# Start-up of a fused convolution and gated feed-forward kernel: w_out scaled on VectorE, w_in loaded for both halves, fp32r remainder of the taps, fillers in the first spread, moved casts, transposes and taps

## Chip, cores, metric

One core of a Trainium2 chip. The metric is the device time of one execution in microseconds (us), lower is better. All runs are compared with runs of the kernel before taken on the same chip in turn.

Three readings of the trace are used throughout, besides the total:

- **T0**: start of the first Silu instruction (ScalarE) of step 0.
- **T1**: start of the first Silu of step 1. Step 0 and step 1 each have 16 half-width Silus.
- **T2**: start of the first full-width Silu, the first of step 2.

## The reference

```python
# x: (8, 4096, 192); weight: (8 heads, 7 taps); w_in: (192, 2048); w_out: (2048, 192)
w = softmax(weight, axis=-1)                 # per head
x_pad = concat([zeros(8, 6, 192), x], axis=1)
conv = sum over k of w[head, k] * x_pad[:, s + k, channels of head]
h = conv.reshape(32768, 192) @ w_in
g = h * sigmoid(beta * h)
out = g @ w_out                              # (32768, 192) float32
```

## The kernel before

Tokens are worked in steps: two of 256 columns (steps 0 and 1), then 31 of 512, each for two halves of the batch at once. In each step a loop over 16 blocks `fc` of the 2048 hidden units issues `hidden` (TensorE, then Silu on ScalarE) for this step and `output` (TensorE) for the step before. Silu is computed as silu(beta h), so w_out is scaled by 1/beta once. VectorE computes the convolution of step s+2 meanwhile: 21 instructions ("taps") per step, taken one by one from a queue at a rate that `pops` sets. The convolutions of steps 0 and 1 are done on TensorE instead, with diagonal matrices, because VectorE would be too late for them. TensorE writes its results to PSUM, a small memory of its own; the kernel takes PSUM in tiles from two pools (`ph` and `po`) of two tiles each, so TensorE must wait when both tiles of a pool are still in use.

```python
w_in_s = consts.tile([128, NG, F], BF16)
def load_w_in(i):                       # to the lower 64 partitions
    nc.gpsimd.dma_start(out=w_in_s[0:DG, :, cols], in_=...)
def copy_w_in(i):                       # to the upper 64
    nc.vector.tensor_copy(w_in_s[DG : 2 * DG, :, cols], w_in_s[0:DG, :, cols])
...
def spread(dst, sel, e8):               # exp(weights), one head a row, to 128 partitions
    for c in range(NG):
        nc.tensor.matmul(dst[...], sel[:, c], e8, start=True, stop=True)
...
fill(5)                                 # matmuls of zeros, to keep TensorE busy
spread(pc[:, 0, :], sel_r, e8r)         # rounded (fp32r) taps, for the diagonal matrices
fill(1)
nc.vector.tensor_copy(eu..., pc[...])
...
def taps():                             # exact taps, for VectorE's convolution
    spread(pq, sel, e8)                 # fp32
    ...
def prep_w_out(c0, n):
    nc.gpsimd.tensor_tensor(w_out_s[...], w_out_raw[...], beta_r[...], ALU.mult)
cast(2)
for c in range(0, NF, 4):
    prep_w_out(c, 4)
cast(3)
...
first_work = {                          # extra work of step 0, by fc
    0: lambda: (first_xt(), taps()),
    2: lambda: (more(xt1_work)(), copy_w_in(1)),   # transposes of the second chunk
    4: lambda: (more(xt1_work)(), copy_w_in(2)),
    6: lambda: (more(conv1_work)(), copy_w_in(3)), # 7 matmuls of step 1's convolution
    8: more(conv1_work),
    11: more(conv1_work),
}
pops = {1: 12, 2: 26}
for s in range(N_ST + 1):
    if s + 2 < N_ST:
        queue.extend(conv_ops(s + 2))
    for u in range(NF):
        if s < N_ST: hidden(s, u)
        if s > 0: output(s - 1, u)
        if s == 0 and u in first_work: first_work[u]()
        n = pops.get(s, 24)
        pops_u = (u + 1) * n // NF - u * n // NF if s else u > 5
        for _ in range(pops_u):
            if queue: queue.popleft()()
        ...
```

## Time and profile before

| | kernel before |
|---|---|
| median of the first 3 runs | 696.64 us |
| profiled span | 695.1 us |
| T0, T1, T2 | 11.84, 25.60, 37.18 us |
| TensorE busy | 687.6 us (99%) |

Busy time of the engines by stage (columns: stage, its length, then busy us and instruction count of each engine). From 60 to 680 us TensorE has no idle time at all, and the change leaves those stages and the last 15 us alone, so only what happens before 60 us can show a difference:

```profile
core 0: us, PE busy (x) PEld busy (x) DVE busy (x) ACT busy (x) POOL busy (x), PEclk, DMA share, GB/s
...
12.00:28.00 16.00, 14.60 (x213) 11.29 (x209) 14.21 (x19) 12.59 (x20) 12.72 (x12) 1.00 1.35 188
28.00:40.00 12.00, 11.68 (x215) 9.90 (x213) 11.93 (x22) 10.97 (x16) 7.01 (x8) 1.00 2.05 155
...
60.00:680.00 620.00, 620.00 (x10440) 474.00 (x10436) 494.01 (x837) 529.06 (x475) 29.87 (x33) 1.00 0.45 70
```

ScalarE's instructions in order of time, merged where they follow each other (columns: start, length, engine and line, operation, shapes, count, and in brackets the idle time before the group and what ended it):

```profile
11.84 0.69 ACT L402 ACTIVATE g<-ph,beta 128x512 bf16<-128x512 f32 x1 [0.37 <-PE ph L395]
13.49 2.55 ACT L402 ACTIVATE g<-ph,beta 128x512 bf16<-128x512 f32 x4 [0.97 <-PE ph L395]
16.25 1.27 ACT L402 ACTIVATE g<-ph,beta 128x512 bf16<-128x512 f32 x2 [0.21 <-PE ph L395]
18.09 1.43 ACT L402 ACTIVATE g<-ph,beta 128x512 bf16<-128x512 f32 x2 [0.57 <-PE ph L395]
20.30 1.97 ACT L402 ACTIVATE g<-ph,beta 128x512 bf16<-128x512 f32 x3 [0.78 <-PE ph L395]
23.05 13.11 ACT L402 ACTIVATE g<-ph,beta 128x512 bf16<-128x512 f32 x20 [0.78 <-PE ph L395]
37.18 5.17 ACT L402 ACTIVATE g<-ph,beta 128x1024 bf16<-128x1024 f32 x5 [1.02 <-PE ph L395]
```

Step 0 is 16 Silus with five gaps; each gap is TensorE doing something else first. Step 1 has no gap; then comes one of 1.02 us. What that one waits for is seen on VectorE, in the same form:

```profile
16.80 3.04 DVE L172 COPY w_in_s<-w_in_s 64x1536 bf16<-64x1536 bf16 x2
19.88 2.92 DVE L376 TENSOR_SCALAR ct<-xt,cw 128x512 bf16<-128x512 bf16 x3
...
31.52 0.55 DVE L456 COPY osb<-po 128x384 f32<-128x384 f32 x1
32.11 0.56 DVE L457 TENSOR_TENSOR osb<-po,osb 128x384 f32<-128x384 f32 x1
32.58 4.06 DVE L378 SCALAR_TENSOR_TENSOR ct<-xt,cw,ct 128x512 bf16<-128x512 bf16 x6
```

The six taps that end at 36.64 are the last of step 2's convolution, and step 2's first matmuls wait for them. Two copies at 16.80 take 3.04 us where one takes 0.69 elsewhere, and three first taps take 2.92 where one takes 0.35: they run beside GpSimd's scaling of w_out (four instructions of 1.57 us, 16.2 to 22.4).

The start of the chain is TensorE's (the first spread is L209, the diagonal matmuls of step 0 are L256):

```profile
3.51 0.80 PE L209 MATMUL po<-e8r,sel_r 8*128 8x8 f32 x3
4.24 0.61 PE L205 MATMUL ph<-zeros 128*128 128x512 bf16 x1
...
6.35 3.36 PE L256 MATMUL ph<-xt_145,diag 128*128 128x256 f32 x14
...
9.85 1.10 PE L256 MATMUL po<-xt_145,diag 128*128 128x256 f32 x7
```

Fourteen matmuls take 0.24 us each, the next seven 0.15: the trace's first record of the full TensorE clock is at 9.90 us. The page's own clock column (PEclk) shows 1.00 from the start, because nothing is recorded before that moment; the matmuls' pace shows that it isn't so.

### The profile page before, as it was taken

What the parts mean: (1) busy time and instruction counts of PE and PEld (TensorE: products, weight loads), DVE (VectorE), ACT (ScalarE), POOL (GpSimd) and SP (SyncE); (2) the same over time, 40 slices, a digit from 0 to 9 for tenths busy, and PEclk for the clock granted to TensorE, in tenths of its full rate; (3) what the DMA queues carried; (4) which work ended last, traced back from release to release, by engine and by line L of the source; (5) the groups of instructions that cost most, each with busy time, mean ns of one, the idle gap of its engine ahead of it and who ended that gap; (6) DMA issues with size and microseconds to landing.
All of it is one profiled execution on the core that took longest, in us unless ns stands there. A gap on an engine that the chain in (4) does not pass through costs nothing.

```text
span 695.1 us, 24865 instructions
## 1 busy us (share of the span) xinstructions
PE 687.6 (99%) x11467; PEld 526.6 (76%) x11467; DVE 551.4 (79%) x938; ACT 580.0 (83%) x546; POOL 70.0 (10%) x83
## 2 busy tenths in 40 slices
PE   9999999999999999999999999999999999999997
PEld 6867777777777777777777777777777777777777
DVE  5999998998777987777987777987778987777222
ACT  6898888888888888888888888888888888888881
POOL 7934455000000000000000000000000000000000
PEclk9999999999999999999999999999999999999999
DMA  9999999922232022222023222032222122211012
GB/s 193 144 159 159 168 177 171 123 63 70 54 65 71 27 68 72 47 70 70 26 71 70 49 70 70 25 71 70 48 71 55 40 70 71 48 48 48 25 48 70
DMA packets 181497, 54.57 MB, mean 79 GB/s; under 512 B 146432, under 2 KB 181072, under 8 KB 181392
## 3 DMA queue, kind: packets, MB, share of 16 engines
q0 software_dynamic: 98048, 14.89, 29.8%
q1 hardware_dynamic: 83296, 38.09, 23.9%
q8 instruction: 89, 1.46, 0.9%
q14 instruction: 16, 0.13, 0.1%
q10 hardware_dynamic: 48, 0.01, 0.0%
HBM read 28.98 MB, written 37.29 MB: 95 GB/s over the span
## 4 chain that ended last, share of the span: by engine, by line
PE 96%; DVE 3%; ACT 0%; issue 0%
PE po L442 48%; PE ph L395 46%; DVE ct L378 2%; PE ph L256 0%; DVE w_in_s L172 0%; DVE ct L376 0%; PE ph L205 0%; PE po L209 0%; PE po L243 0%; ACT g L402 0%; PE po L256 0%; DVE xt L346 0%; DVE osb L457 0%; DVE ct L327 0%; ACT xt_145 L269 0%
## 5 line engine op out<-in xcount | busy, mean ns | idle before, releaser
L402 ACT ACTIVATE g<-ph,beta 128x1024 bf16<-128x1024 f32 (+1 forms) x528 | 572.7, 1090 | 96.7 <-PE ph L395 92.6
L442 PEld LDWEIGHTS <-g 64*128 64x128 bf16 x8192 | 369.2, 94 | 101.9
L442 PE MATMUL po<-w_out_s,g 64*128 64x192 bf16 x8192 | 429.8, 243 | 0.0
L395 PE MATMUL ph<-ct,w_in_s 64*128 64x512 bf16 (+1 forms) x3168 | 426.2, 370 | 2.0 <-ACT g L402 1.1
L378 DVE SCALAR_TENSOR_TENSOR ct<-xt,cw,ct 128x512 bf16<-128x512 bf16 x558 | 379.4, 745 | 0.0
L395 PEld LDWEIGHTS <-w_in_s 64*128 64x128 bf16 x3168 | 162.5, 94 | 56.4 <-issue 2.9
L456 DVE COPY osb<-po 128x384 f32<-128x384 f32 x127 | 70.8, 558 | 126.9 <-PE po L442 120.7
L457 DVE TENSOR_TENSOR osb<-po,osb 128x384 f32<-128x384 f32 x129 | 71.5, 555 | 6.0 <-ACT osb L454 1.6
L95 POOL DMA_DIRECT2D xd<-in_x_dram x60 | 54.4, 909 | 46.1 <-DMA xd<-in_x_dram 42.3
L376 DVE TENSOR_SCALAR ct<-xt,cw 128x512 bf16<-128x512 bf16 x93 | 29.5, 372 | 0.0
L454 ACT COPY osb<-po 128x192 f32<-128x192 f32 x2 | 0.6, 320 | 9.9 <-PE po L442 9.9
L352 POOL TENSOR_TENSOR w_out_s<-w_out_raw,beta_r 128x768 bf16<-128x768 f32 x4 | 6.2, 1568 | 2.5 <-DMA w_out_raw<-in_moe_w_out_dram 2.5
L205 PE MATMUL ph<-zeros 128*128 128x512 bf16 x7 | 3.5, 623 | 1.3 <-DVE warm L129 1.3
L172 DVE COPY w_in_s<-w_in_s 64x1536 bf16<-64x1536 bf16 x4 | 4.4, 1121 | 0.1
L256 PE MATMUL po<-xt_145,diag 128*128 128x256 f32 x28 | 4.4, 296 | 0.0
L256 PEld LDWEIGHTS po<-xt_145,diag 128*128 128x128 f32 x28 | 3.6, 189 | 0.7 <-issue 0.6
L256 PEld LDWEIGHTS ph<-xt_145,diag 128*128 128x128 f32 x14 | 3.1, 327 | 0.6 <-ACT xt_145 L269 0.6
L256 PE MATMUL ph<-xt_145,diag 128*128 128x256 f32 x14 | 3.4, 427 | 0.1
L185 POOL DMA_DIRECT2D w_out_raw<-in_moe_w_out_dram x4 | 3.1, 771 | 0.3 <-DMA x1b<-in_x_dram 0.3
L295 ACT ACTIVATE ct<-po,rn 128x256 bf16<-128x256 f32 x1 | 0.5, 475 | 2.6 <-PE po L256 2.6
L165 POOL DMA_DIRECT2D w_in_s<-in_moe_w_in_dram x4 | 2.7, 669 | 0.0
L205 PEld LDWEIGHTS <-zeros 128*128 128x128 bf16 x7 | 0.8, 126 | 2.3 <-DVE warm L129 1.3
(51 smaller groups left out, 28.1 us busy)
## 6 DMA issues: line engine op xcount, KB each, us to landing
out_dram<-osb SPq DMA_DIRECT2D x60, 384.0 KB, 3.1
xd<-in_x_dram POOLq DMA_DIRECT2D x54, 198.0 KB, 14.5
w_out_raw<-in_moe_w_out_dram POOLq DMA_DIRECT2D x4, 384.0 KB, 9.4
out_dram<-osb SPq DMA_DIRECT2D x7, 192.0 KB, 3.7
xd<-in_x_dram POOLq DMA_DIRECT2D x6, 192.0 KB, 13.7
x_83<-in_x_dram SPq DMA_DIRECT2D x4, 192.0 KB, 2.9
w_in_s<-in_moe_w_in_dram POOLq DMA_DIRECT2D x4, 192.0 KB, 7.7
xt<-xd SPq DMA_TRANSPOSE x30, 5.1
```

The costliest lines, as they stand in the source:

```text
L95: nc.gpsimd.dma_start(out=xd[r0:, :, h, :], in_=x_v[p, t0:t1, h, :].rearrange("t (c d) -> t c d", c=NG),)
L172: nc.vector.tensor_copy(w_in_s[DG : 2 * DG, :, cols], w_in_s[0:DG, :, cols])
L205: nc.tensor.matmul(pf[:, 0, :], zeros[:, 0:128], zeros, start=True, stop=True)
L256: nc.tensor.matmul(pv, diag[:, c, k, :], xt0[:, c, o : o + n], start=(k == 0), stop=(k == K - 1),)
L352: nc.gpsimd.tensor_tensor(w_out_s[:, c0 : c0 + n, :], w_out_raw[:, c0 : c0 + n, :], beta_r[:, c0 : c0 + n].unsqueeze(2).to_broadcast((128, ...
L376: nc.vector.tensor_scalar_mul(dst, src, scalar)
L378: nc.vector.scalar_tensor_tensor(out=dst, in0=src, scalar=scalar, in1=dst, op0=ALU.mult, op1=ALU.add)
L395: nc.tensor.matmul(ph[:, h, 0:n], w_in_s[rows, j, cols], cts[s][rows, j, 0:n], start=(j == 0), stop=(j == NG - 1),)
L402: nc.scalar.activation(gs[s][:, fc, :, 0:n], ph[:, :, 0:n], AF.Silu, scale=beta[:, fc : fc + 1])
L442: nc.tensor.matmul(po[:, r, b * D : (b + 1) * D], g[rows, fc, h, q * BLK : (q + 1) * BLK], w_out_s[rows, fc, :], start=(fc == 0), stop=(fc ...
L456: nc.vector.tensor_copy(dst, po[:, 0, cols])
L457: nc.vector.tensor_tensor(dst, po[:, 1, cols], dst, ALU.add)
```

## The change

Its intent is to relieve VectorE and ScalarE in the start-up: GpSimd no longer computes beside VectorE (it goes on issuing DMAs), two of VectorE's four w_in copies become DMA, the exact taps come from cheap fp32r matmuls on the remainder e8 - e8r, added to the rounded taps, the late x rows are cast where VectorE idles, and the first spread is kept "busy" by three small matmuls of zeros ("fillers"). The same edit rearranges step 0: the second chunk's transposes move from fc 2 and 4 to fc 1 and 2, and VectorE takes 7 taps from the queue in step 0 (10 before) and 15 in step 1 (12 before). So 13 of step 2's 21 taps stand ahead of step 1's first output copy, where 15 did.

```diff
-    def load_w_in(i):
+    def load_w_in(i, h=0):
...
-    for i in range(1, NW):
-        load_w_in(i)
+    load_w_in(1)
+    for i in range(2, NW):
+        for h in range(2):
+            load_w_in(i, h)
...
-    def spread(dst, sel, e8):
+    def spread(dst, sel, e8, between=0):
         for c in range(NG):
+            fill(between, 128)
...
+    e8l = setup.tile([H, K + 1], FP32R)
+    nc.vector.tensor_tensor(e8l, e8, e8r.bitcast(FP32), ALU.subtract)
     fill(5)
-    spread(pc[:, 0, :], sel_r, e8r)
+    spread(pc[:, 0, :], sel_r, e8r, between=1)
...
     diag_v(1)
+    nc.vector.tensor_copy(x0b[:, HB:NB], x0[:, HB:NB])
...
-        spread(pq, sel, e8)
+        spread(pq, sel_r, e8l)
+        ef = setup.tile([128, NG, K + 1], FP32)
+        nc.vector.tensor_tensor(ef, pq..., eu, ALU.add)
...
-        nc.gpsimd.tensor_tensor(          # w_out scaling
+        nc.vector.tensor_tensor(
...
     first_work = {
-        0: lambda: (first_xt(), taps()),
-        2: lambda: (more(xt1_work)(), copy_w_in(1)),
-        4: lambda: (more(xt1_work)(), copy_w_in(2)),
-        6: lambda: (more(conv1_work)(), copy_w_in(3)),
-        8: more(conv1_work),
-        11: more(conv1_work),
+        (0, 0): lambda: (first_xt(), taps()),
+        (0, 1): lambda: (more(xt1_work)(), copy_w_in(1)),
+        (0, 2): more(xt1_work),
+        (0, 5): more(conv1_work),
+        (0, 6): lambda: cast(3),
+        (0, 8): more(conv1_work),
+        (0, 11): lambda: (prep_w_out(0), prep_w_out(4), more(conv1_work)()),
+        (0, 13): lambda: prep_w_out(8),
+        (0, 14): lambda: prep_w_out(12),
+        (0, 15): lambda: cast(4),
     }
-    pops = {1: 12, 2: 26}
+    pops = {1: 15, 2: 24}
...
-            pops_u = (u + 1) * n // NF - u * n // NF if s else u > 5
+            pops_u = (u + 1) * n // NF - u * n // NF if s else 2 < u < 10
```

More of the change, by code (lines that the diff above doesn't have):

```diff
@@ L161 @@
     w_in_s = consts.tile([128, NG, F], BF16)
-    def load_w_in(i):
+    def load_w_in(i, h=0):
         cols = slice(i * FW, (i + 1) * FW)
         nc.gpsimd.dma_start(
-            out=w_in_s[0:DG, :, cols],
+            out=w_in_s[h * DG : (h + 1) * DG, :, cols],
             in_=moe_w_in[:, cols].rearrange("(c d) f -> d c f", c=NG),
@@ L201, with fill @@
     pf = psum_h.tile([128, 2, TOK], FP32, name="ph")
-    def fill(n):
+    def fill(n, cols=TOK):
         for _ in range(n):
-            nc.tensor.matmul(pf[:, 0, :], zeros[:, 0:128], zeros, start=True, stop=True)
-    def spread(dst, sel, e8):
+            nc.tensor.matmul(
+                pf[:, 0, 0:cols], zeros[:, 0:128], zeros[:, 0:cols], start=True, stop=True
+            )
+    def spread(dst, sel, e8, between=0):
         for c in range(NG):
+            fill(between, 128)
             nc.tensor.matmul(
@@ L295 @@
             nc.scalar.mul(ct[:, c, 0:n0], pv, rn[:, c : c + 1])
-    beta_r = setup.tile([128, NF], FP32)
-    nc.vector.reciprocal(beta_r, beta)
-    nc.vector.tensor_copy(x0b[:, HB:NB], x0[:, HB:NB])
     cw = consts.tile([128, NG, K], FP32)
@@ L304, in taps @@
         pq = psum_o.tile([128, 2, TOK], FP32, name="po")[:, 0, 0 : NG * (K + 1)]
-        spread(pq, sel, e8)
-        pq = pq.rearrange("p (c k) -> p c k", c=NG)
+        spread(pq, sel_r, e8l)
+        ef = setup.tile([128, NG, K + 1], FP32)
+        nc.vector.tensor_tensor(ef, pq.rearrange("p (c k) -> p c k", c=NG), eu, ALU.add)
         rq = setup.tile([128, NG], FP32)
-        nc.vector.reciprocal(rq, pq[:, :, K])
+        nc.vector.reciprocal(rq, ef[:, :, K])
         nc.vector.tensor_tensor(
-            cw, pq[:, :, 0:K], rq.unsqueeze(2).to_broadcast((128, NG, K)), ALU.mult
+            cw, ef[:, :, 0:K], rq.unsqueeze(2).to_broadcast((128, NG, K)), ALU.mult
         )
@@ L349, with prep_w_out @@
     w_out_s = consts.tile([128, NF, D], BF16)
-    def prep_w_out(c0, n):
-        nc.gpsimd.tensor_tensor(
-            w_out_s[:, c0 : c0 + n, :],
-            w_out_raw[:, c0 : c0 + n, :],
-            beta_r[:, c0 : c0 + n].unsqueeze(2).to_broadcast((128, n, D)),
+    beta_r = setup.tile([128, NF], FP32)
+    def prep_w_out(c):
+        if c == 0:
+            nc.vector.reciprocal(beta_r, beta)
+        nc.vector.tensor_tensor(
+            w_out_s[:, c : c + 4, :],
+            w_out_raw[:, c : c + 4, :],
+            beta_r[:, c : c + 4].unsqueeze(2).to_broadcast((128, 4, D)),
             ALU.mult,
@@ L359 @@
     cast(2)
-    for c in range(0, NF, 4):
-        prep_w_out(c, 4)
-    cast(3)
     def conv_ops(s):
@@ L486 @@
                 output(s - 1, u)
-            if s == 0 and u in first_work:
-                first_work[u]()
+            if (s, u) in first_work:
+                first_work[s, u]()
             n = pops.get(s, 24)
-            pops_u = (u + 1) * n // NF - u * n // NF if s else u > 5
+            pops_u = (u + 1) * n // NF - u * n // NF if s else 2 < u < 10
             for _ in range(pops_u):
@@ L493 @@
                     queue.popleft()()
-            if u == 0 and s + 4 < N_CH:
+            if u == 0 and 0 < s < N_CH - 4:
                 cast(s + 4)
```

## The prediction

> **What bounds it now.** TensorE is busy for 687.6 of 695.1 us, and from 60 to 680 us for all of every window (busy time by stage). The change leaves those stages alone; only the start-up counts. From the instructions in order of time:
> - The first Silu starts at 11.84 us. The 32 half-width Silus of the first two steps take 0.66 us each.
> - Step 0 (16 Silus) lasts until 25.60: 16 x 0.65 plus ScalarE gaps of 0.97, 0.21, 0.57, 0.78, 0.78 us. The last three follow blocks of seven convolution matmuls (1.05 us).
> - Step 1 runs at 0.657 us per Silu to 36.15, then ScalarE idles 0.96 us: step 2's hidden matmuls wait for VectorE's last convolution tap (done 36.64).
> - Step 2 is ScalarE's (1.014 us each), to 53.4; then TensorE's.
>
> So at most 4-5 us can be had, 0.7%.
>
> **What the change does, costed.**
> 1. w_out scaling leaves GpSimd (4 x 1.57 us, 16.2 to 22.4). Meanwhile two w_in copies took 1.43 and 1.68 us instead of 0.69, and two k=0 taps 1.18 and 1.55 instead of 0.29. The Trainium skill ("SBUF — State Buffer", shared port pair) says that GpSimd and a VectorE instruction in a two-port mode exclude each other; this trace agrees, with about 3.9 us lost. VectorE pays instead 4 x about 0.9 us (estimate from diag, 896 fp32 elements in 1.06 us).
> 2. Two w_in copies (0.69 each undisturbed) go; two loads of 192 KB come. Estimate: w_out and the first cast land about 2 us later, still before use.
> 3. The exact taps: six fp32 passes (0.76 us) become three fp32r matmuls, about 0.4 us at full clock, shortening the 0.97 gap by 0.4. Two small VectorE additions: 0.3 us.
> 4. Three fillers in the first spread: eu about 0.2 us later, at half clock. But the granted clock reaches full only at 9.90 us, after 14 diagonal matmuls at 0.24 us instead of 0.15. "TensorE: Matmul & The Clock Gate", Part 1, says that a busy window of about 3.4 us lifts the gate. If the fillers make an earlier window count, about 1.0 us is saved; I give that 40%.
> 5. The late x cast moves into a gap at 7.14-8.25: nothing, since the transposes did not wait for it.
>
> **On the critical path.** VectorE's relief is 3.5-4 us net, but most of it does not arrive. VectorE will reach step 1's first output copy before TensorE has finished that output (start of step 1 + 4.9 us), wait about 1 us, and then still have that pair (1.06) and 8 taps (0.66 each), part of which stood ahead of it before. So step 2 starts about 11.8 us after step 1, against 11.58 now: the stall there stays, with another cause. Step 0 gets about 0.5 us shorter, mostly from item 3. Item 4 is worth -0.2 to +1.0. Sum: 0.2 to 1.8 us gained, about 0.9.
>
> **Predicted: 695.7 us, range 694.0 to 697.0.** Faster by over 2%: 0.005; within 2%: 0.99; slower by over 2%: 0.005.
>
> **What would show it.** Copies and k=0 taps at 0.69 and 0.29 us throughout; w_out scaling 0.9 us on VectorE; the taps' spread near 0.4 us; ScalarE's three conv gaps still 0.6-0.8; the first 1024-wide Silu at about 36.3 (now 37.18) after ScalarE idled near 1 us; VectorE idle before the first output copy; full clock at 6.5 (gain) or 9.9 us; the stages from 60 us equal.
>
> **What would make it wrong.** VectorE reaching that copy late, so that the relief pays in full: 693-694. Or the extra loads and earlier casts delaying a transposed x chunk that step 1 or 2 needs: 697-698. Or the clock gate opening later, by its own phase.

## The result and the profile after

| | before | after |
|---|---|---|
| median (range), 4 runs each | 696.43 us (696.14 to 696.79) | 697.58 us (697.48 to 698.66) |
| profiled span | 695.1 us | 697.0 us |
| eu (rounded taps copied on VectorE) | 4.35 us | 5.06 us |
| first record of the full clock | 9.90 us | 11.56 us |
| T0 | 11.84 us | 12.98 us |
| T1 - T0 | 13.76 us | 14.17 us |
| T2 - T1 | 11.58 us | 11.92 us |
| T2 to the end | 657.9 us | 657.9 us |

The ratio is 1.002 with an interval of 1.0002 to 1.0037: slower by about 1.2 us, which is clear of noise. Ratios here are the mean time of one kernel's runs over that of the other's of the same rounds, so not quite the ratio of the medians quoted. The predicted 695.7 us (694.0 to 697.0) was wrong in size and in sign.

In the two profiled runs T2 is 1.89 us later, and the rest is the same, so all of the loss lies before T2. First the busy time by stage of the changed kernel; the long stage is as full as before, the stages from 12 to 40 us are emptier on TensorE:

```profile
12.00:28.00 16.00, 13.55 (x187) 10.09 (x188) 12.98 (x22) 11.79 (x19) 12.16 (x14) 1.00 1.84 215
28.00:40.00 12.00, 11.39 (x225) 10.31 (x222) 10.67 (x19) 10.66 (x16) 3.94 (x5) 1.00 1.79 157
...
60.00:680.00 620.00, 620.00 (x10434) 475.06 (x10430) 497.40 (x842) 528.49 (x475) 28.91 (x32) 1.00 0.44 70
```

TensorE's start in the changed kernel (L214 is the spread, L207 the fillers, L263 the diagonal matmuls):

```profile
3.61 0.37 PE L214 MATMUL po<-e8r,sel_r 8*128 8x8 f32 x1
3.92 0.29 PE L207 MATMUL ph<-zeros 128*128 128x128 bf16 x1
4.13 0.37 PE L214 MATMUL po<-e8r,sel_r 8*128 8x8 f32 x1
4.44 0.29 PE L207 MATMUL ph<-zeros 128*128 128x128 bf16 x1
4.66 0.37 PE L214 MATMUL po<-e8r,sel_r 8*128 8x8 f32 x1
4.96 0.61 PE L207 MATMUL ph<-zeros 128*128 128x512 bf16 x1
...
7.07 3.36 PE L263 MATMUL ph<-xt,diag 128*128 128x256 f32 x14
```

A spread matmul followed by a filler takes 0.52 us, where spread matmuls alone followed each other at 0.22 to 0.24. The diagonal matmuls start at 7.07 us instead of 6.35. Then ScalarE:

```profile
12.98 0.69 ACT L408 ACTIVATE g<-ph,beta 128x512 bf16<-128x512 f32 x1 [0.37 <-PE ph L401]
14.30 0.69 ACT L408 ACTIVATE g<-ph,beta 128x512 bf16<-128x512 f32 x1 [0.63 <-PE ph L401]
15.46 0.69 ACT L408 ACTIVATE g<-ph,beta 128x512 bf16<-128x512 f32 x1 [0.47 <-PE ph L401]
16.34 1.97 ACT L408 ACTIVATE g<-ph,beta 128x512 bf16<-128x512 f32 x3 [0.20 <-PE ph L401]
19.09 1.97 ACT L408 ACTIVATE g<-ph,beta 128x512 bf16<-128x512 f32 x3 [0.78 <-PE ph L401]
21.84 1.97 ACT L408 ACTIVATE g<-ph,beta 128x512 bf16<-128x512 f32 x3 [0.79 <-PE ph L401]
24.59 9.82 ACT L408 ACTIVATE g<-ph,beta 128x512 bf16<-128x512 f32 x15 [0.78 <-PE ph L401]
35.16 3.32 ACT L408 ACTIVATE g<-ph,beta 128x512 bf16<-128x512 f32 x5 [0.74 <-PE ph L401]
39.07 3.14 ACT L408 ACTIVATE g<-ph,beta 128x1024 bf16<-128x1024 f32 x3 [0.60 <-PE ph L401]
```

The first gap of step 0 shrank from 0.97 to 0.63 us, as the three fp32r passes promised, but a gap of 0.47 us is new and the first convolution gap grew from 0.57 to 0.78. The gap of 0.74 us at 35.16 follows a stall of 0.54 us on TensorE in step 1 (to 34.29) whose cause the trace does not name; a second profile of the same kernel (e5_again) has no such stall and the same T2 - T1, so it cost nothing. And VectorE:

```profile
20.98 1.83 DVE L361 TENSOR_TENSOR w_out_s<-w_out_raw,beta_r 128x768 bf16<-128x768 f32 x2
...
26.76 4.06 DVE L384 SCALAR_TENSOR_TENSOR ct<-xt,cw,ct 128x512 bf16<-128x512 bf16 x6
32.08 0.56 DVE L462 COPY osb<-po 128x384 f32<-128x384 f32 x1 [1.26 <-PE po L448]
32.68 0.56 DVE L463 TENSOR_TENSOR osb<-po,osb 128x384 f32<-128x384 f32 x1
33.15 5.38 DVE L384 SCALAR_TENSOR_TENSOR ct<-xt,cw,ct 128x512 bf16<-128x512 bf16 x8
```

VectorE now stands idle for 1.26 us before the first output copy of step 1, with eight taps still to come behind it that need nothing of that copy. Before, six stood behind it and there was no idle time before it. The eight end at 38.53, and step 2's first matmuls start at 38.58: T2 waits for them.

How much VectorE was relieved can be added up. From T0 to the end of step 2's last tap VectorE was busy for 22.81 us before and 22.21 us after (`--windows 11.84:36.64` and `--windows 12.98:38.53`). So the relief is 0.60 us net: the contention and two copies went, but four scalings of 0.95 us came. Its idle time in that stretch grew from 1.99 to 3.34 us.

### The profile page after: what moved, and what is told of

It reads as the page before. It is cut to its first block, busy times and chain, and to the rows that moved or that the text cites. A ratio compares the mean times of both kernels' runs of the same rounds, so it can differ in the third digit from the quotient of the medians.

```text
span 697.0 us, 24867 instructions
## 1 busy us (share of the span) xinstructions
PE 688.4 (99%) x11467; PEld 528.5 (76%) x11467; DVE 551.2 (79%) x942; ACT 579.5 (83%) x546; POOL 65.0 (9%) x81
## 3 DMA queue, kind: packets, MB, share of 16 engines
q8 instruction: 89, 1.46, 0.9%
## 4 chain that ended last, share of the span: by engine, by line
PE 97%; DVE 1%; ACT 1%; issue 0%
PE po L448 48%; PE ph L401 47%; DVE ct L384 1%; PE po L263 1%; ACT g L408 1%; PE ph L207 0%; PE ph L263 0%; PE po L250 0%; DVE xt L323 0%; DVE osb L463 0%; PE po L214 0%; ACT xt L276 0%; DVE osb L462 0%; ACT ct L303 0%; ACT osb L460 0%
## 5 line engine op out<-in xcount | busy, mean ns | idle before, releaser
L207 PE MATMUL ph<-zeros 128*128 128x512 bf16 (+1 forms) x10 | 4.2, 525 | 1.3 <-DVE warm L129 1.3
L263 PE MATMUL po<-xt,diag 128*128 128x256 f32 x28 | 4.8, 316 | 0.0
L263 PEld LDWEIGHTS po<-xt,diag 128*128 128x128 f32 x28 | 4.0, 211 | 0.7 <-issue 0.6
L361 DVE TENSOR_TENSOR w_out_s<-w_out_raw,beta_r 128x768 bf16<-128x768 f32 x4 | 3.6, 953 | 0.0
L263 PEld LDWEIGHTS ph<-xt,diag 128*128 128x128 f32 x14 | 3.1, 328 | 0.6 <-ACT xt L276 0.6
L263 PE MATMUL ph<-xt,diag 128*128 128x256 f32 x14 | 3.4, 427 | 0.1
L207 PEld LDWEIGHTS <-zeros 128*128 128x128 bf16 x10 | 1.2, 124 | 2.6 <-issue 1.3
```

The lines of the kernel that those rows point to most:

```text
L207: nc.tensor.matmul(pf[:, 0, 0:cols], zeros[:, 0:128], zeros[:, 0:cols], start=True, stop=True)
L263: nc.tensor.matmul(pv, diag[:, c, k, :], xt0[:, c, o : o + n], start=(k == 0), stop=(k == K - 1),)
L361: nc.vector.tensor_tensor(w_out_s[:, c : c + 4, :], w_out_raw[:, c : c + 4, :], beta_r[:, c : c + 4].unsqueeze(2).to_broadcast((128, 4, D) ...
```

## The experiments

Twelve runs were made, in three calls (each on a chip of its own), five rounds each, all correct. Since the moment at which the full clock begins differs from run to run, T0 of single profiles is not compared directly; T1 - T0 and T2 - T1 repeat within 0.02 us for the same kernel (the changed one and e5_again, e7_combo and e12_combo2) and are compared instead. The kernel before has one profile only. Each call has nine runs of the kernel before (medians 696.53, 696.49 and 696.41 us).

### e1_nofill: the changed kernel without the three fillers

```diff
-    spread(pc[:, 0, :], sel_r, e8r, between=1)
+    spread(pc[:, 0, :], sel_r, e8r)
```

> The changed kernel without the three fillers in the first spread. Theory A (the fillers are paid on the start-up chain, 0.5 us a pair instead of 0.22): eu at 4.35-4.4 us instead of 5.06, the first Silu about 0.7 us earlier, total 696.9 (changed kernel: 697.6). Rival B (fillers bring the clock gate forward and are worth their time): the same or slower than the changed kernel, first record of the full clock later than with fillers. What stays above the kernel before (0.4-0.5 us) would be the order of step 0 and step 1.

Inconclusive. The profiled execution took 4118.2 us; the other four 696.8 to 697.8 (median of all 697.56), which is no gain that four runs could tell. In the slow execution TensorE was the one engine that was busy all the time:

```profile
PE 4111.1 (100%) x11464; PEld 1853.5 (45%) x11464; DVE 550.7 (13%) x942; ACT 582.0 (14%) x546; POOL 65.1 (2%) x81
```

VectorE and ScalarE needed their usual time, TensorE six times its own, and the trace holds no record of its clock at all. It is one execution of sixty in these experiments and is left out of every comparison. The kernel was run again as e6_nofill2.

### e2_fill_only: the kernel before with only the fillers

```diff
-    spread(pc[:, 0, :], sel_r, e8r)
+    spread(pc[:, 0, :], sel_r, e8r, between=1)
```

> The kernel before with only the three fillers. Theory A: eu at 5.0-5.1 us, 0.7 us slower than before (697.1). Rival B: no slower than before, as the full clock comes earlier. If both act, between the two.

Median 697.21 us, 0.68 over the kernel before; eu at 5.06 us. Theory A's numbers were met, though the interval of the ratio (0.9996 to 1.0021) includes 1. (In its profile step 0 was 14.30 us long, 0.54 more than in the kernel before with the same order; an extra gap on TensorE there ends 0.1 us after a 16 KB transfer of the instruction queue. That is a coincidence of one profile and not followed up.) T2 - T1 was 10.90 us there, against 11.58, so T2 - T0 was 25.20 against 25.34: in the order of before T2 waits for VectorE, and what step 0 loses step 1 can win back. For the kernel before T2 - T0 is therefore the safer figure: 25.34 us, against 26.09 in the changed kernel.

### e3_late_xt1: the second chunk's transposes one fc later

```diff
-        (0, 1): lambda: (more(xt1_work)(), copy_w_in(1)),
+        (0, 1): lambda: copy_w_in(1),
         (0, 2): more(xt1_work),
+        (0, 3): more(xt1_work),
```

> The changed kernel with the transposes of the second chunk one fc later (2 and 3 instead of 1 and 2). Theory: at fc 1 they wait for the PSUM tile that VectorE's cast of the first chunk still holds (done 14.40); one fc later that wait is gone, the ScalarE gap of 0.47 us after the second Silu shrinks to about 0, and step 1 starts 0.2-0.4 us earlier after the first Silu (14.17 now); total 697.2-697.4. Rival (the step is bound by TensorE's sum, the place does not matter): unchanged within 0.1.

Median 697.03 us. The 0.47 gap is gone and the first convolution gap is back at 0.58:

```profile
13.15 1.97 ACT L408 ACTIVATE g<-ph,beta 128x512 bf16<-128x512 f32 x3 [0.63 <-PE ph L401]
15.33 1.27 ACT L408 ACTIVATE g<-ph,beta 128x512 bf16<-128x512 f32 x2 [0.21 <-PE ph L401]
17.18 1.97 ACT L408 ACTIVATE g<-ph,beta 128x512 bf16<-128x512 f32 x3 [0.58 <-PE ph L401]
```

T1 - T0 fell from 14.17 to 13.40 us, twice what was expected; T2 - T1 stayed at 11.92. In the changed kernel the transposes at fc 1 have to wait for a PSUM tile: the pool has two, one taken by the taps' spread and one still held by VectorE's cast (12.30 to 13.26 in the kernel before, 13.44 to 14.40 in the changed one):

```profile
13.44 0.96 DVE L323 CAST xt<-po 128x768 fp32r<-128x768 bf16 x1 [2.41 <-PE po L250]
14.45 0.53 PE L250 MATMUL po<-ident_b,x1b 128*64 128x128 bf16 x12 [0.20 <-DVE xt L323]
```

At fc 2 the tile is free. The wait itself is 0.20 us of TensorE. The rest of the 0.77 us is not attributed: e3 also let two blocks of hidden matmuls run back to back before the first transposes, so that ScalarE had a Silu in reserve. The place cost 0.77 us; how much of it is the tile is not shown.

### e4_pops: the pops of before

```diff
-    pops = {1: 15, 2: 24}
+    pops = {1: 12, 2: 24}
-            ... if s else 2 < u < 10
+            ... if s else 2 < u < 13
```

> The changed kernel with the pops of before (10 taps in step 0, 12 in step 1): 12 taps stand before the first output copy of step 1 instead of 10, 6 after it instead of 8. Theory: VectorE's idle time of 1.26 us before that copy goes, and the first full-width Silu comes 0.8-1.3 us earlier after the start of step 1 (11.92 in the changed kernel, to 10.8-11.1); total 696.3-696.8, about the kernel before. Rival (VectorE is simply overloaded by the w_out scaling): no idle before the copy but the last tap as late as now, total 697.5.

T2 - T1 fell from 11.92 to 11.04 us with T1 - T0 unchanged at 14.16, as expected; the idle time before the copy fell to 0.60, not to zero. The median, 697.14 us, is 0.3 above the expected range (one run of the five took 698.23), and 0.4 below the changed kernel's (measured in another call). The last tap of step 2 now ends 24.22 us after T0, against 24.80 in the kernel before and 25.55 in the changed one.

### e5_again and e6_nofill2: the control, and again without fillers

> The changed kernel unaltered, as control on this chip and for a second look at the clock gate. Expected: eu at 5.06 us, step 0 14.1-14.2 us from first Silu to step 1's first, step 1 to step 2 11.92; first Silu between 11.7 and 13.0 us, according to where the full clock begins: from the five profiles so far, 0.41 us later for each us that the clock opens later. Total 697.0-698.3, median near 697.5.

> The changed kernel without the fillers again (the first look fell into an execution at about a sixth of the speed). Theory A: eu at 4.35-4.4; first Silu 0.71 us earlier than the line through the runs with fillers at a clock opening 0.71 us later (for example 11.84 for an opening at 9.9); median 0.4-0.7 below the control of the same call. Rival B (fillers pay for themselves through the gate): the clock opens a whole window later than in the runs with fillers (8.6 to 11.6 so far) and the median is not below the control.

Control: median 698.17 us, T1 - T0 14.16, T2 - T1 11.92. Without fillers: 697.39, so 0.78 us less, eu at 4.34. Theory A was met, rival B was not: the clock opened at 9.25 us, not a window later. All profiles together, by the first record of the full clock:

| fillers | full clock at / T0 (us) |
|---|---|
| with | 8.60/11.75, 8.80/11.84, 9.68/12.21, 10.34/12.48, 10.57/12.55, 11.56/12.98 |
| without | 4.74/10.48, 7.92/11.04, 7.98/11.08, 9.25/11.63, 9.90/11.84, 10.06/11.92, 10.56/12.14 |

Leaving out the 4.74, each row is a straight line with a slope of 0.41 us of T0 for a us of clock, within 0.04 us; at the same opening the fillers cost 0.42 us, and with an opening that comes later by the 0.71 us that the diagonal matmuls do, all of 0.71. The medians (0.68 and 0.78 us) are nearer to the second, but their scatter does not exclude the first. The one early opening (4.74) came in a kernel without fillers.

The clock records tell more. The stretch at full clock lasts 682.67, 686.08 or 689.49 us in the 13 profiles that have one, which is 200, 201 and 202 times 3.41 us: the gate opens and closes on a beat of 3.41 us. To gain time the fillers had to make the beat before count. In the six profiles with fillers that beat fell between 5.19 us (8.60 - 3.41) and 8.15 us (11.56 - 3.41), and the clock did not open at it in any of them.

### e7_combo: e1's, e3's and e4's edits at once

> The changed kernel without fillers, with the transposes of the second chunk one fc later, and with the pops of before. If the three losses add up: eu 4.35, step 0 13.4 us long, step 1 to step 2 10.9-11.1 (24.4 from first Silu to the first full-width one, against 25.34 before and 26.09 changed); 1.7 us below the control after correction for the clock's opening, about 0.8 below the kernel before: 695.5-696.0. Rival (they share one wait): no more than 1 us below the control.

Median 695.72 us: 2.45 below the control and 0.77 below the kernel before, T1 - T0 13.40, T2 - T1 10.90. The three losses add up (0.71 + 0.77 + 0.88 = 2.36). In the profile:

```profile
21.92 13.11 ACT L408 ACTIVATE g<-ph,beta 128x512 bf16<-128x512 f32 x20 [0.78 <-PE ph L401]
35.38 5.17 ACT L408 ACTIVATE g<-ph,beta 128x1024 bf16<-128x1024 f32 x5 [0.35 <-PE ph L401]
```

The gap before T2 is 0.35 us where it was 1.02 before.

### e8_gpsimd: w_out scaled on GpSimd in the changed kernel

```diff
     def prep_w_out(c):
-        nc.vector.tensor_tensor(
+        nc.gpsimd.tensor_tensor(
...
     cast(2)
+    for c in range(0, NF, 4):
+        prep_w_out(c)
```

> The changed kernel with the w_out scaling put back on GpSimd. Theory: VectorE is not what bounds step 1 there, the wait for the first output copy is; so VectorE's idle time before that copy grows from 1.26 to 3 us or more unless GpSimd stretches the taps beside it, and the first Silu of step 2 still comes 11.9 us after step 1's: total within 0.3 of the control. Rival (the scaling on VectorE is what costs): 1 us or more faster than the control.

Median 698.02 us, 0.15 from the control; T1 - T0 14.16 and T2 - T1 11.92, the same. VectorE:

```profile
17.38 7.58 DVE L386 SCALAR_TENSOR_TENSOR ct<-xt,cw,ct 128x512 bf16<-128x512 bf16 x4
...
31.64 0.56 DVE L464 COPY osb<-po 128x384 f32<-128x384 f32 x1 [1.84 <-PE po L450]
```

Four taps took 1.95 us each beside GpSimd, instead of 0.74. The Trainium skill ("SBUF — State Buffer", shared port pair) says that a VectorE instruction with two SBUF inputs, as these taps are, contends with a GpSimd one that reads SBUF, and this trace agrees. VectorE was about as loaded either way, the idle time before the copy was even longer, and T2 - T1 did not move: in the changed kernel's order the place of the scaling is worth nothing.

### e9_split and e10_split_w1: the convolution matmuls in smaller pieces; one more w_in piece loaded

```diff
 # e9_split, on e7_combo: 21 matmuls in pieces of 3 at fc 4 to 9 and 11
-        for c in range(NG):
-            for k in range(K):
-                diag_tap(1, c, k, pv[:, c, :])
+        for i in range(NG * K):
+            c, k = divmod(i, K)
+            diag_tap(1, c, k, pv[:, c, :])
...
+            if i % 3 == 2:
+                yield
 # e10_split_w1, on e9_split
-    load_w_in(1)
-    for i in range(2, NW):
+    for i in range(1, NW):
...
-        (0, 1): lambda: copy_w_in(1),
```

> e7_combo with the 21 convolution matmuls of step 0 in seven pieces of three, at fc 4 to 9 and 11, in place of three blocks of seven. Theory: the three ScalarE gaps of 0.58-0.79 us are TensorE's blocks of 1.05 us; in pieces of 0.45 us each costs 0.1-0.2, step 0 shortens from 13.40 to 12.2-12.6, but VectorE's chain then ends last: first full-width Silu 23.4-23.7 us after the first Silu, against 24.30 in e7_combo. Total 0.6-0.9 us below e7_combo, 694.8-695.2. Rival (TensorE's sum bounds step 0): step 0 stays at 13.4.

> e9_split with the second w_in piece loaded for both halves too, so that its VectorE copy of 0.69 us goes. If VectorE's chain is the last in e9_split, another 0.5-0.7 us earlier (22.8-23.0 us from first Silu to first full-width one), total 694.2-694.7; if the piece lands too late, a ScalarE gap appears before the fifth Silu and the total is above e9_split.

Both expectations failed. e9_split: 695.99 us, T1 - T0 13.28, T2 - T1 10.90; e10_split_w1: 695.97 us, the same two. Three gaps of 0.58 to 0.79 became six of 0.30, and step 0 stayed, as the rival said: in e9_split TensorE is busy for all of the stretch with the pieces (15.41 to 22.03 us). TensorE and its weight loads in e9_split (columns as before; PEld is the weight load):

```profile
15.85 0.50 PE L402 MATMUL ph<-ct,w_in_s 64*128 64x256 bf16 x6
16.28 0.63 PE L263 MATMUL po<-xt,diag 128*128 128x256 f32 x3
16.84 0.50 PE L402 MATMUL ph<-ct,w_in_s 64*128 64x256 bf16 x6
```

```profile
16.28 0.41 PEld L263 LDWEIGHTS po<-xt,diag 128*128 128x128 f32 x3 [0.21 <-issue]
16.84 0.22 PEld L402 LDWEIGHTS <-w_in_s 64*128 64x128 bf16 x6
```

A round of hidden matmuls and three diagonal ones takes 0.99 us, against 0.66 for a Silu, and every change from 64-row bf16 weights to 128-row fp32r ones comes with 0.21 us in which no weights are loaded (so does the change to the 128-row bf16 weights of the transposes). A block of seven takes TensorE 1.03 us in e7_combo and a block of three 0.55 us here, which makes, as an estimate from these two, 0.2 us for a block and 0.12 for each matmul. Cutting the blocks finer pays the 0.2 more often; from e7_combo to e9_split TensorE's idle time in step 0 fell from 1.63 to 0.55 us, and its busy time rose from 11.77 to 12.73 us. And as step 0 did not shorten, VectorE never became the last, so taking a copy from it (e10) gained nothing.

### e11_fp32_taps and e12_combo2: the fp32 taps back in e7_combo, and its control

```diff
-        spread(pq, sel_r, e8l)
-        ef = ...
-        nc.vector.tensor_tensor(ef, pq..., eu, ALU.add)
+        spread(pq, sel, e8)
+        ef = pq...
```

> e7_combo with the exact taps spread in fp32 again (six passes) in place of the fp32r remainder. Theory: the first ScalarE gap of step 0 goes back from 0.63 to 0.96 us, step 0 from 13.40 to 13.7; total 0.2-0.4 above e7_combo's control of this call. Rival (that gap is hidden by later ones): step 0 unchanged.

> e7_combo again, as the control of this call: step 0 13.40 us, 24.3 us from first Silu to first full-width one, total 695.0-696.1, and below the kernel before by 0.5-1.0 us.

As expected: with fp32 taps the first gap is 0.97 again and T1 - T0 13.74 instead of 13.40; median 696.15 against the control's 695.75. So this part of the change is worth 0.34 us. e12_combo2 repeats e7_combo: 695.75 us, 0.66 below the kernel before. The interval of e12's ratio is 0.9976 to 1.0001 and of e7's 0.9977 to 1.0004, so each interval alone just includes 1; together the ten runs average 0.89 us below the eighteen of the kernel before in the same calls, and the traces show where the gain comes from.

## Why the prediction was wrong

**What failed: the fillers.** "Three fillers in the first spread: eu about 0.2 us later, at half clock", with a 40% chance of 1.0 us saved through the clock gate. Measured: 0.71 us later (e2, and every profile with fillers). The prediction does not say how it came to 0.2; the trace shows 0.52 us for a filler and a spread matmul, where the spread matmul alone took 0.22 to 0.24. The saving did not come: with fillers the full clock began between 8.6 and 11.6 us, without them between 4.7 and 10.6, and in none of the six profiles with fillers did it begin a beat earlier. The Trainium skill ("TensorE: Matmul & The Clock Gate", Part 1) says that the activity window runs freely and does not restart with the kernel. The spread of the openings for one and the same kernel agrees (9.68 and 11.56 in the changed one, 4.74 and 7.98 in e7_combo), as if the phase were chance. What level of activity makes a window count is not settled here.

**What failed: step 0.** "Step 0 gets about 0.5 us shorter, mostly from item 3." It got 0.41 us longer. Item 3 itself was right in mechanism and nearly in size (0.34 us, e11). But the same edit of the table moved the second chunk's transposes from fc 2 and 4 to fc 1 and 2; this cost 0.77 us (e3). At fc 1 they wait 0.20 us for a PSUM tile that VectorE still holds, and they stand ahead of hidden matmuls for which ScalarE then waits 0.47 us; e3 undoes both together. The prediction costed what was added and removed and never asked what the moved transposes would wait for and hold up, though the two tiles of the pool stand in the kernel and the length of VectorE's cast in its profile.

**What failed: the size of VectorE's relief.** "VectorE's relief is 3.5-4 us net". It was 0.60 us (22.81 to 22.21 us busy from T0 to the last tap). The contention had cost 3.9 us and the two copies 1.4; but the scaling took 3.8, and the rest went to small additions. The predicted T2 - T1 did not suffer, as it was worked out from the copy and the taps behind it and not from the relief.

**What held: step 1.** "The stall there stays, with another cause": T2 - T1 was predicted at about 11.8 us and was 11.92; VectorE's predicted idle time of about 1 us before the first output copy was 1.26. e4 shows that the cause is the pops: two more taps ahead of the copy bring 0.88 us. e8 agrees: there VectorE was 0.6 us earlier at the copy (idle for 1.84 us instead of 1.26), and T2 - T1 changed by nothing.

**What held: the contention and the DMAs.** Scaling took 0.95 us per instruction on VectorE (0.9 expected), and the copies were back at 0.69. The taps were at 0.35 except for one of 0.71. The extra loads delayed nothing that anybody waited for. The moved cast gained nothing that shows. The stages from 60 us are equal.

The sum: the prediction had about 0.9 us gained from -0.2 to +1.0 (fillers), +0.5 (step 0) and -0.2 (step 1), terms that add up to 0.1 to 1.3 and not to its 0.2 to 1.8. In the traces it was -0.71, -0.41 and -0.34, in all 1.46 us lost. The remaining 0.43 of the 1.89 us between the two profiles is the clock gate, which opened 1.66 us later in the profiled run. The medians (1.15 us in the first runs, 1.68 in e5's call) lie around 1.46, as T0's dependence on the gate lets one expect.

**Where VectorE's relief went.** GpSimd's contention had cost VectorE about 3.9 us, and its removal is real, but the scaling took its place, and 0.60 us were left. The 1.35 us of idle time that came between T0 and the last tap (1.99 to 3.34) are not relief: they are as long as the two taps (1.3 us) that the new pops put behind the copy instead of ahead of it. With the old pops (e4) the idle time is back at 2.00 us, and the last tap comes 0.58 us earlier after T0 than in the kernel before, which is nearly the whole relief. With all three edits (e7) T2 - T1 is 10.90 us, and T2 no longer waits for a tap: the last one ends at 34.52 and T2 is at 35.38.

## What to carry to other kernels

Before counting on a relief, subtract what the engine has to do instead; here 3.9 us became 0.6. An in-order engine waits at the first instruction that another engine must feed, so keep work that is independent of it ahead of it; two taps on the wrong side cost 0.88 us here. When a change moves work to another place, ask which buffer it needs there and who holds it, as carefully as one counts what was added. A filler on the critical chain cost close to its full time here, and a clock that opens by a free-running window makes single runs differ by more than such details are worth: compare intervals between events, not totals of single runs.

## What the Trainium skill lacked or had wrong

- "TensorE: Matmul & The Clock Gate", Part 1, describes the gate's window but not what a filler costs between small matmuls: an 8-row fp32r matmul with a 128-column bf16 filler behind it took 0.52 us at the low clock, such fp32r matmuls alone followed each other at 0.22 to 0.24 us.
- The same page, "LDWEIGHTS (loading the stationary operand)", gives column count over 1.2 (107 ns for 128 columns, an estimate from that formula) with no figure for fp32r: here 14 such loads took 328 ns on average before the full clock (they overlap, and their matmuls follow each other at 240 ns). Nor does it give a time for the change from 64-row to 128-row weights: here 0.21 us without a load, before fp32r and bf16 weights alike (e9_split).
- The same page, Part 1, has seen the gate stuck low for over 50 us; one execution of sixty here had TensorE busy for 4111 us of 4116, six times its usual time, from start to end and without any clock record. Whether that was the gate is not shown.
